# Attention and two mixture-of-experts layers: first expert's weights loaded at its choice, second unit of the second layer fixed one group earlier

## The chip, the cores and the metric

The kernel runs on one core of a Trainium2 chip. That core has TensorE (PE, matrix multiplication), VectorE (DVE), ScalarE (ACT), GpSimd (POOL) and SyncE (SP), which execute their own instruction rows in order and wait for one another by semaphores, and DMA engines that move data between the chip's memory and the core's. The metric is the time of one execution in microseconds (us); lower is better.

## The reference

Attention in two steps over 8 batches, 8 heads and 576 tokens gives x with 4608 rows of 512. Two layers of 8 experts follow. In the first, each expert takes at most 576 tokens, in the order of falling logits; in the second, a token goes to the expert with its largest logit, however many others do.

```python
def _moe_ref(x, w_gate, w1, w2):
    cap = N // E
    logits = x @ w_gate
    order = np.argsort(-logits.flatten())
    for idx in order:
        tok, e = (int(idx) // E, int(idx) % E)
        if assigned[tok] >= 0 or counts[e] >= cap:
            continue
        assigned[tok] = e
        counts[e] += 1
    for e in range(E):
        mask = assigned == e
        out[mask] = np.maximum(x[mask] @ w1[e], 0.0) @ w2[e]

def _moe2_ref(x, modality_id, w_gate, modality_bias, w1, w2):
    logits = x @ w_gate + modality_bias[modality_id]
    e_idx = np.argmax(logits, axis=1)
    gate_w = softmax(logits)[np.arange(N), e_idx]
    for e in range(E):
        mask = e_idx == e
        out[mask] = gate_w[mask, None] * (np.maximum(x[mask] @ w1[e], 0.0) @ w2[e])
```

Here w1 is 512 x 1024 and w2 1024 x 512 for each expert. For these inputs, worked out from the reference, the second layer sends 2308 tokens to one expert and 2300 to another.

## The kernel before

**Attention** handles one batch after the other. ScalarE copies each batch's result to `xm` in five pieces, and five DMAs on SP's row store them to the memory tensor `xs` (L372). The logits of the first layer are made on the way (`LG`), so the routing of the first layer can begin before the last batches are stored.

**Routing of the first layer** runs in eight phases (`class Phases`). Phase k chooses the expert whose list fills next (`choose`, the register tile `R.ex`) and then makes the list of its 576 tokens. A list that fills is found by search steps: VectorE compares (`ge`), TensorE counts (`b`, L654), VectorE folds (`two`, `cp`). `early` (called in attention's last iteration) is the part of the search that needs only the first 20 of the 36 tiles of logits: seven VectorE operations, `best`, `rw`, `mxc`, `sign`, `key`, `digits`.

**Units.** Each expert of the first layer is a unit of 576 tokens (units 0 to 7). The second layer's lists are cut into units of 580 tokens; for these inputs there are eight, called E to E+7 here after their numbers in the code (E is 8). A unit has its weights loaded by SP to the landing tile `raw`, 4 chunks for each of its two weight matrices (L1407, L1428), which are split into a high and a low part by ScalarE (`w1H`, `w2H`, L1460) and mostly VectorE (`w1L`, `w2L`, L1466). GpSimd gathers its tokens to `G` by indirect DMAs (L1263 and L1282), they are transposed to `XT` and split to `XH` and `XL`. Then come the first matrix (`mm`, L1517, three products for each piece), relu and its split `hH` (ScalarE, L1492) and `hL` (VectorE, L1494), the second matrix (L1572), and a store (first layer, `ys`) or an indirect scatter (second layer, `out_dram`, L1344).

**Second layer's lists.** After each expert of the first layer, its 576 results are a "group": the second layer's logits are made, each token is put on the list of its best expert in memory (`lst`, five indirect writes on GpSimd, L973), and counts are kept. `R2.first` fixes unit E after seven of the eight groups: it takes the longest list. After the eighth group `R2.table` places all the other units: an iota on GpSimd (L876), then 24 small VectorE operations, t_s to t_b (L877 to L913). `prepare` loads a unit's expert and list from memory: SP loads `M` and `Mb`, VectorE turns them to gather indices `gi` and scatter indices `si`.

**Order.** The rows of all engines are written out in advance. A planner (`Sched`) holds chains of operations (`cx`, `cw`, `cm` and others), each with a due time, and puts them between the matmuls as its own clock advances. An engine that waits holds all that stands behind it in its row.

Of the kernel before, what the change touches and what calls it, by code (L numbers as in the profile page):

```python
# [59 lines left out]
def attention(tc, ctx, cn, q, k, v, p, w_gate, xs, LG, middle, early):  # L60
# [300 lines left out]
    def out_rows(b, c, ring, hook=None):  # L361
        ahead(b, c)
        n = 128 if c < 4 else 64
        dst = wk.tile([128, 4, 4, 32], F32, name="xm", bufs=5)[:n]
        t = ring.tile([128, 4, 4, 32], F32, name="tr")[:n]
        for g in range(2):
            nc.tensor.matmul(t[:, 2 * g:2 * g + 2], aT[b][:, g, 128 * c:128 * c + n], ops[b][:, g], start=True, stop=True)  # L367
            if hook and not g:
                hook()
        nc.scalar.activation(dst, t.rearrange("p c a i -> p a c i"), AF.Copy)  # L370
        to = xs[b * S:b * S + 512].rearrange("(p m) d -> m p d", m=4)[c] if c < 4 else xs[b * S + 512:(b + 1) * S]
        nc.sync.dma_start(to, dst.rearrange("p a c i -> p (a c i)"))  # L372
        if c == 4:
            del aT[b], ops[b]
# [27 lines left out]
    for i in range(B):  # L402
# [43 lines left out]
        if p1 and SM == 1:  # L446
            sm_max(i - 1)
            sm_sub(i - 1, nc.gpsimd)
        if EARLY and not n1 and EP == 1:
            early()  # L450
        pack_v(i)
        fill(FILL[2])
        pack_D(i)
        if p2 and AT == 0:
            sm_aT(i - 2)
        if AP == 2:
            ahead(*todo[0])
# [156 lines left out]
class Router:  # L614
# [206 lines left out]
class Router2:  # L821
# [39 lines left out]
    def first(self):  # L861
        nc, cn, new = self.nc, self.cn, self.new
        m, t = new("f_m", [128, 1]), new("f_t", [128, E])
        self.fcode, self.fi = new("f_c", [128, 1]), new("f_i", [128, 2], I32)
        nc.vector.tensor_reduce(m, self.cnt, axis=AX.X, op=OP.max)
        nc.vector.scalar_tensor_tensor(t, self.cnt, m, cn["w8"], op0=OP.is_equal, op1=OP.mult)
        nc.vector.tensor_reduce(self.fcode, t, axis=AX.X, op=OP.max)
        self.again = new("f_r", [128, 1])
        nc.vector.tensor_scalar(self.again, m, float(IT), None, op0=OP.is_lt)
        nc.vector.tensor_scalar(self.fi[:, 0:1], self.fcode, -1.0, float(E), op0=OP.mult, op1=OP.add)  # L870
        nc.vector.tensor_scalar(self.fi[:, 1:], self.fcode, -float(LCAP), float(E * LCAP), op0=OP.mult, op1=OP.add)

# [260 lines left out]
EP = 1  # L1133
# [5 lines left out]
RLAG = 2.6  # L1139
IT = 580  # L1140
IG = (IT + 31) // 32
HB = 256
HA = IT - HB
GA = (HA + 31) // 32
RING = 5
NI = (N + E * (IT - 1)) // IT + 1
LCAP = N + -(-IG // 2) * 64


def forward(tc, ctx, cn, R, R2, wg2, S, P, todo, rows, closing, xs, ys, lst, out, m1_w1, m1_w2, m2_w1, m2_w2):  # L1150
    nc = tc.nc
# [9 lines left out]
    def more_phases():  # L1161
        k = phase_k[0]
        if k < E and k <= min(started[0] + 3, P.coded + 2):
            phase_k[0] += 1
            P.add(k)

    for b, c in todo:
# [7 lines left out]
    W = {n: wp.tile([128, 4096], F32R, name="w" + n) for n in ("1H", "1L", "2H", "2L")}  # L1175
    raw = wp.tile([128, 4, 1024], F32, name="raw")
    raws = [raw[:, i] for i in range(4)]
    mp = ctx.enter_context(tc.tile_pool(name="m_ps", bufs=1, space=PSUM))
# [17 lines left out]
    gathered, l1_done, lg_done = [0], [-1], [-1]  # L1196
    free = list(raws)
    queue = []
    landed, due = {}, {}

    class Unit:
# [11 lines left out]
        def ready(self):  # L1213
            if self.one:
                return self.u in P.experts
            return groups[0] >= (7 if self.u == E else 8) and (self.u < E + RING or finished[0] >= self.u - RING)

        def prepare(self):
# [3 lines left out]
            if self.one:  # L1222
                t, i = R.ex, self.u
            elif self.u == E:
                R2.first()
                t, i = R2.fi, 0
            else:
                t, i = R2.tb[:, 0], self.u - E
            self.e = nc.values_load(t[0:1, i:i + 1], engines=[SP], min_val=0, max_val=E - 1)
            if not self.one:  # L1230
                t, i = (R2.fi, 1) if self.u == E else (R2.tb[:, 1], self.u - E)
                off = nc.values_load(t[0:1, i:i + 1], engines=[SP], min_val=0, max_val=(E - 1) * LCAP + N)
# [15 lines left out]
                if self.last:  # L1248
                    cm.ops.append(("vector", 0.1, lambda: nc.vector.tensor_copy(sa, Ma[:, :, 1]), t))
            for which in (1, 2):  # L1250
                queue.extend((self, which, c) for c in range(4))
# [6 lines left out]
        def gather(self):  # L1258
# [139 lines left out]
    def fetch():  # L1398
        while queue and free:
            u, which, c = queue[0]  # L1400
            w = ((m1_w1, m1_w2) if u.one else (m2_w1, m2_w2))[which - 1]
            if which == 1 and (not u.u or 2 <= u.u < BYROW):
                queue.pop(0)
                t = free.pop(0)
                rows = w[bass.ds(u.e, 1)].rearrange("o (c a i) f -> a c i (o f)", a=4, i=32)[c]
                for i in range(4):
                    nc.sync.dma_start(t[32 * i:32 * i + 32], rows[i])  # L1407
                landed[u.u, which, c] = t
                due[u.u, which, c] = S.t["sync"] = max(S.t["sync"], S.t["tensor"] + (2 if u.u else LAND)) + 2.2
                continue  # L1410
# [279 lines left out]
def tile_attention_moe(ctx, tc, q, k, v, p, m1_wg, m1_w1, m1_w2, mod_id, m2_wg, m2_bias, m2_w1, m2_w2, out):  # L1690
# [30 lines left out]
    P.add(0)  # L1721
    forward(tc, ctx, cn, R, R2, wg2, S, P, todo, rows, attn.close, xs, ys, lst, out, m1_w1, m1_w2, m2_w1, m2_w2)

# [21 lines left out]
```

## Time and profile before

| what | value |
|---|---|
| median of 3 runs | 1134.14 us (1133.48 to 1136.73) |
| profiled execution | 1134.52 us |
| its span | 1132.8 us |
| TensorE busy | 1041.8 us, 92% of the span |
| VectorE / GpSimd / ScalarE busy | 713.5 / 488.7 / 444.6 us |
| chain: TensorE, VectorE, issue, DMA, GpSimd | 60%, 12%, 9%, 9%, 5% |
| mean granted clock of TensorE | 0.976 of full |

The span reaches from the first to the last recorded instruction. Busy shares are means over stages with different limits. The chain is followed back from the last instruction, each step to what released it.

### The profile page before, as it was taken

What the parts mean: (1) busy time and instruction counts of PE and PEld (TensorE: products, weight loads), DVE (VectorE), ACT (ScalarE), POOL (GpSimd) and SP (SyncE); (2) the same over time, 40 slices, a digit from 0 to 9 for tenths busy, and PEclk for the clock granted to TensorE, in tenths of its full rate; (3) what the DMA queues carried; (4) which work ended last, traced back from release to release, by engine and by line L of the source; (5) the groups of instructions that cost most, each with busy time, mean ns of one, the idle gap of its engine ahead of it and who ended that gap; (6) DMA issues with size and microseconds to landing.
All of it is one profiled execution on the core that took longest, in us unless ns stands there. A gap on an engine that the chain in (4) does not pass through costs nothing.

```text
span 1132.8 us, 24490 instructions
## 1 busy us (share of the span) xinstructions
PE 1041.8 (92%) x9152; PEld 967.9 (85%) x9152; DVE 713.5 (63%) x2105; ACT 444.6 (39%) x940; POOL 488.7 (43%) x595
## 2 busy tenths in 40 slices
PE   6689797699899998999999999989999999999996
PEld 4577664588888897989999999979898999999995
DVE  1468777688979889884556566655555556455430
ACT  4467564323332323333434334333443433434331
POOL 1123301212424224047565344477787778742401
PEclk9899899699999999999999999999999999999998
DMA  9989246633243242224345343554445454433301
GB/s 257 278 228 259 53 168 201 158 75 117 64 139 113 80 137 57 99 89 145 117 134 138 99 145 93 135 143 126 126 144 143 106 170 136 127 125 102 99 20 43
DMA packets 117857, 146.90 MB, mean 130 GB/s; under 512 B 55946, under 2 KB 80522, under 8 KB 116704
## 3 DMA queue, kind: packets, MB, share of 16 engines
q1 hardware_dynamic: 102368, 116.43, 35.9%
q0 software_dynamic: 13776, 28.76, 8.7%
q8 instruction: 74, 1.21, 0.5%
q14 instruction: 55, 0.45, 0.2%
q10 hardware_dynamic: 1584, 0.05, 0.1%
HBM read 116.31 MB, written 29.52 MB: 129 GB/s over the span
## 4 chain that ended last, share of the span: by engine, by line
PE 60%; DVE 12%; issue 9%; DMA 9%; POOL 5%; ACT 2%; SPq 2%; POOLq 0%; ACTq 0%; DVEq 0%
PE mm L1572 26%; PE mm L1517 22%; DMA G<-ys,gi 4%; POOL out_dram L1344 3%; PE sc L170 2%; POOL G L1282 2%; PE tr L367 1%; DMA raw<-in_moe_w_dram 1%; PE sc L367 1%; DVE hL L1494 1%; DMA G<-xs,idx 1%; DMA vm<-in_v_dram 1%; PE tr L150 1%; DVE cmx L1008 1%; PE b L150 1%
## 5 line engine op out<-in xcount | busy, mean ns | idle before, releaser
L1517 PE MATMUL mm<-XH,w1H 128*128 128x290 f32 (+3 forms) x1024 | 306.9, 300 | 8.7 <-ACT XH L1301 3.8
L1517 PE MATMUL mm<-XL,w1H 128*128 128x290 f32 (+3 forms) x1024 | 307.9, 301 | 0.5 <-DVE XL L1321 0.3
L1517 PE MATMUL mm<-XH,w1L 128*128 128x290 f32 (+3 forms) x1024 | 305.4, 298 | 2.8 <-DVE w1L L1466 2.7
L1572 PE MATMUL mm<-hH,w2H 128*128 128x288 f32 (+3 forms) x768 | 231.9, 302 | 1.1 <-ACT YT L1577 1.1
L1572 PE MATMUL mm<-hH,w2L 128*128 128x288 f32 (+3 forms) x768 | 232.7, 303 | 0.0
L1572 PE MATMUL mm<-hL,w2H 128*128 128x288 f32 (+3 forms) x768 | 231.7, 302 | 0.1
L1492 ACT ACTIVATE hH<-mm 128x290 fp32r<-128x290 f32 (+3 forms) x256 | 105.7, 413 | 293.4 <-PE mm L1517 279.6
L1517 PEld LDWEIGHTS mm<-XH,w1H 128*128 128x128 f32 x1024 | 195.2, 191 | 11.2 <-ACT XH L1301 4.2
L1517 PEld LDWEIGHTS mm<-XH,w1L 128*128 128x128 f32 x1024 | 195.4, 191 | 3.9 <-DVE w1L L1466 3.5
L1517 PEld LDWEIGHTS mm<-XL,w1H 128*128 128x128 f32 x1024 | 194.7, 190 | 1.6 <-DVE XL L1321 0.8
L1494 DVE SCALAR_TENSOR_TENSOR hL<-mm,hH 128x290 fp32r<-128x290 f32 (+3 forms) x256 | 115.2, 454 | 116.7 <-ACT hH L1492 115.6
L1282 POOL DMA_INDIRECT G<-ys,gi x152 | 158.2, 1041 | 62.8 <-issue 31.7
L1572 PEld LDWEIGHTS mm<-hH,w2H 128*128 128x128 f32 x768 | 144.5, 188 | 1.6 <-ACT YT L1577 1.5
L1572 PEld LDWEIGHTS mm<-hL,w2H 128*128 128x128 f32 x768 | 144.5, 188 | 0.3 <-DVE hL L1494 0.3
L1572 PEld LDWEIGHTS mm<-hH,w2L 128*128 128x128 f32 x768 | 144.4, 188 | 0.1
L1344 POOL DMA_INDIRECT out_dram<-Y,si x93 | 96.1, 1033 | 112.0 <-DVE Y L1542 48.5
L1466 POOL TENSOR_TENSOR w2L<-raw,w2H 128x512 fp32r<-128x512 f32 x48 | 63.2, 1338 | 172.2 <-ACT w2H L1460 172.1
L1577 ACT ACTIVATE YT<-mm 128x288 f32<-128x288 f32 (+2 forms) x96 | 39.9, 419 | 203.8 <-PE mm L1572 202.1
L1308 DVE STREAM_TRANSPOSE XT<-G 128x128 f32<-128x128 f32 x206 | 55.6, 295 | 83.6 <-DMA G<-ys,gi 62.0
L1466 DVE TENSOR_TENSOR w1L<-raw,w1H 128x512 fp32r<-128x512 f32 x128 | 83.8, 677 | 19.6 <-ACT w1H L1460 19.0
L1460 ACT ACTIVATE w1H<-raw 128x512 fp32r<-128x512 f32 x128 | 73.1, 623 | 19.5 <-DMA raw<-in_moe_w_dram 11.5
L1460 ACT ACTIVATE w2H<-raw 128x512 fp32r<-128x512 f32 x128 | 73.1, 622 | 0.0
(383 smaller groups left out, 1544.3 us busy)
## 6 DMA issues: line engine op xcount, KB each, us to landing
raw<-in_moe_w_dram SPq DMA_DIRECT2D x112, 512.0 KB
ys<-Y SPq DMA_DIRECT2D x8, 1152.0 KB
qm<-in_q_dram SPq DMA_DIRECT2D x8, 1024.0 KB
vm<-in_v_dram SPq DMA_DIRECT2D x8, 1024.0 KB
xs<-xm SPq DMA_DIRECT2D x32, 256.0 KB
raw<-in_moe_w_dram SPq DMA_DIRECT2D x64, 128.0 KB
km<-in_k_dram SPq DMA_DIRECT2D x7, 1024.0 KB
G<-ys,gi POOLq DMA_INDIRECT x152
```

Of the source, the lines that this page charges most:

```text
L150: nc.tensor.transpose(t[:, i, :], src[:, h + i // 2, 128 * (i % 2):128 * (i % 2) + 128], ident)
L170: nc.tensor.matmul(t[32 * c:32 * c + 32, :512].rearrange("p (i j n) -> p j i n", i=2, j=2)[:, j], lhs(h, j), m[:, h], start=True, stop=Tru ...
L1282: nc.gpsimd.indirect_dma_start(out=G[:, g], out_offset=None, in_=ys[:n], in_offset=bass.IndirectOffsetOnAxis(ap=self.gi[:, g:g + 1], axis= ...
L1308: nc.vector.transpose(out=self.x[0][:, :, 32 * g:32 * g + 32], in_=G[:, g].rearrange("p (c i) -> p c i", c=4))
L1344: i = nc.gpsimd.indirect_dma_start(out=to, in_=rows, in_offset=None, out_offset=bass.IndirectOffsetOnAxis(ap=at, axis=0), bounds_check=to. ...
L1460: nc.scalar.activation(a, b, AF.Copy)
L1466: (nc.gpsimd if pool else nc.vector).tensor_tensor(p[0], p[1], p[2], op=OP.subtract)
L1492: nc.scalar.activation(hh, t, AF.Relu)
L1494: ch.ops.append(("vector", 0.37, lambda: nc.vector.scalar_tensor_tensor(hl, t, 0.0, hh.bitcast(F32), op0=OP.max, op1=OP.subtract), ts + 0.2))
L1517: nc.tensor.matmul(t, a[:, c, fs], b[:, c, s], start=(i == 0), stop=(i == 11))
L1572: nc.tensor.matmul(t, l, r, start=(i == 0), stop=(i == 23))
L1577: nc.scalar.activation(YT[:, d, s], t, AF.Copy)
```

## The change

Four things are edited. First, `raw` is taken from a pool that exists all the time, not from one opened after attention is closed; a hook on `choose` (`first_loads`) issues unit 0's 16 first-matrix loads on SP as soon as the first expert is chosen, and the five stores of the last batch go from SP's row to ScalarE's. Second, `early` is called behind `pack_v`, `pack_D` and `sm_aT`. Third, `PRE = 2`: `R2.first` fixes two units after seven groups, E and the next 580 tokens of the same list (for these inputs the lists of both experts hold 2016 tokens then, so `again`, which would void the early choice on a short list, stays zero), and `prepare` and the gathers of E+1 follow E's; its gathers read only the rows of the first seven groups. Fourth, with one more unit that may be needed, `NI` grows from 16 to 17, and the rows of the table from 128 to 136 numbers.

```diff
-        nc.sync.dma_start(to, dst.rearrange("p a c i -> p (a c i)"))
+        (nc.scalar if b == B - 1 else nc.sync).dma_start(to, dst.rearrange("p a c i -> p (a c i)"))
...
-        if EARLY and not n1 and EP == 1:
-            early()
         pack_v(i)
         fill(FILL[2])
         pack_D(i)
         if p2 and AT == 0:
             sm_aT(i - 2)
+        if EARLY and not n1 and EP == 1:
+            early()
...
+        for i in range(2, PRE + 1):
+            nc.vector.scalar_tensor_tensor(self.again, m, float(IT * i), self.again, op0=OP.is_lt, op1=OP.add)
...
+        for i in range(PRE):
+            nc.vector.tensor_scalar(self.fi[:, 1 + i:2 + i], self.fcode, -float(LCAP), float(E * LCAP + IT * i), op0=OP.mult,
+                                    op1=OP.add)
...
+PRE = 2
...
-NI = (N + E * (IT - 1)) // IT + 1
+NI = (N + E * (IT - 1)) // IT + PRE
...
+    def load_rows(u, e, c, t):
+        w = m1_w1 if u < E else m2_w1
+        rows = w[bass.ds(e, 1)].rearrange("o (c a i) f -> a c i (o f)", a=4, i=32)[c]
+        for i in range(4):
+            nc.sync.dma_start(t[32 * i:32 * i + 32], rows[i])
+        landed[u, 1, c] = t
+        due[u, 1, c] = S.t["sync"] = max(S.t["sync"], S.t["tensor"] + (2 if u else LAND)) + 2.2
+
+    def first_loads():
+        if one_e or 0 not in P.experts:
+            return
+        one_e.append(nc.values_load(R.ex[0:1, 0:1], engines=[SP], min_val=0, max_val=E - 1))
+        for c in range(4):
+            load_rows(0, one_e[0], c, raws[c])
+
+    P.hooks.append(first_loads)
...
-    raw = wp.tile([128, 4, 1024], F32, name="raw")
-    raws = [raw[:, i] for i in range(4)]
...
-            return groups[0] >= (7 if self.u == E else 8) and (self.u < E + RING or finished[0] >= self.u - RING)
+            return groups[0] >= (7 if self.u < E + PRE else 8) and (self.u < E + RING or finished[0] >= self.u - RING)
...
-                t, i = (R2.fi, 1) if self.u == E else (R2.tb[:, 1], self.u - E)
+                t, i = (R2.fi, 1 + self.u - E) if self.u < E + PRE else (R2.tb[:, 1], self.u - E)
...
-                t = S.t["tensor"] + (CM0 if self.u == E else CM1)
+                t = S.t["tensor"] + (CM0 if self.u < E + PRE else CM1)
...
-            n = 4 * (N - CAP if self.u == E else N)
+            n = 4 * (N - CAP if self.u < E + PRE else N)
...
-            if g > E and g + 1 < limit[0]:
+            if g >= E and g + 1 < limit[0]:
                 units[g + 1].prepare()
...
+    raw = rp.tile([128, 4, 1024], F32, name="raw")
```

Line numbers move by the change (L1466 becomes L1483, L1494 becomes L1511, L1282 becomes L1304). The rows below are read without times: they are the order of the instructions.

SP's row at the end of attention, before: the stores of the last two batches (L372), then the load of the chosen expert's number and the first weights (L1407).

```order
L372 DMA xs<-xm 128x512 x4
L372 DMA xs<-xm 64x512
L372 DMA xs<-xm 128x512 x4
L372 DMA xs<-xm 64x512
L1229 TENSOR_LOAD ex
L1229 ISA x2
L1407 ISA
L1407 DMA raw<-in_moe_w_dram 32x1024
```

After the change, at the same place:

```order
L372 DMA xs<-xm 128x512 x4
L372 DMA xs<-xm 64x512
L372 DMA xs<-xm 128x512 x4
L372 DMA xs<-xm 64x512
L1186 TENSOR_LOAD ex
L1186 ISA x2
L1179 ISA
L1179 DMA raw<-in_moe_w_dram 32x1024
```

The last batch's five stores have left the row, and the weights follow the stores of the batch before it.

GpSimd's row at the second layer's start, before: the gathers of E (`gi_2490`), the last group's five list writes, two of which stand here, the iota, the gathers of E+1 (`gi_2491`), the first scatter of E.

```order
L1282 DMA G<-ys,gi_2490 128x128 x19
L973 DMA lst<-pay,r2d 41984x4
L975 MEMSET spacer 1x1
...
L973 DMA lst<-pay,r2d 41984x4
L975 MEMSET spacer 1x1
L876 IOTA t_i 1x16
L1282 DMA G<-ys,gi_2491 128x128 x19
L1344 DMA out_dram<-Y,si_2495 18432x128
```

After the change (`gi_2516` is E, `gi_2517` is E+1, `gi_2513` is E+2):

```order
L1304 DMA G<-ys,gi_2516 128x128 x19
L1304 DMA G<-ys,gi_2517 128x128 x19
L977 DMA lst<-pay,r2d 41984x4
L979 MEMSET spacer 1x1
...
L977 DMA lst<-pay,r2d 41984x4
L979 MEMSET spacer 1x1
L880 IOTA t_i 1x17
L1304 DMA G<-ys,gi_2513 128x128 x19
```

E+1's gathers have moved ahead of the five list writes and the iota; behind the iota now stand E+2's gathers, which were behind twelve of E's scatters.

VectorE's row while unit E is in its first matrix, before: the eighth of the sixteen `hL` of this matrix, the table from `t_s` to `t_b`, and the three `hL` that follow it.

```order
L1494 SCALAR_TENSOR_TENSOR hL<-mm_2464,hH 128x290
L1466 TENSOR_TENSOR w2L<-raw,w2H 128x4x4x32
L877 TENSOR_SCALAR t_s<-t_i 1x16
L878 TENSOR_SCALAR t_e<-w_351 1x8
...
L913 CAST t_b<-t_y 1x32
L1466 TENSOR_TENSOR w2L<-raw,w2H 128x4x4x32
L1494 SCALAR_TENSOR_TENSOR hL<-mm_2465,hH 128x290
L1494 SCALAR_TENSOR_TENSOR hL<-mm_2466,hH 128x290
L1494 SCALAR_TENSOR_TENSOR hL<-mm_2467,hH 128x290
```

After the change:

```order
L1483 TENSOR_TENSOR w2L<-raw,w2H 128x4x4x32
L1511 SCALAR_TENSOR_TENSOR hL<-mm_2489,hH 128x290
L881 TENSOR_SCALAR t_s<-t_i 1x17
L882 TENSOR_SCALAR t_e<-w_352 1x8
...
L917 CAST t_b<-t_y 1x34
L1511 SCALAR_TENSOR_TENSOR hL<-mm_2490,hH 128x290
L1511 SCALAR_TENSOR_TENSOR hL<-mm_2491,hH 128x290
L1511 SCALAR_TENSOR_TENSOR hL<-mm_2492,hH 128x290
L1549 MEMSET YT 128x4x28
```

The table has moved down to between the thirteenth and the fourteenth `hL` of unit E; three of the sixteen stand behind it, where eight stood before.

## Rows read from the trace of the kernel before

**Rows 1.** The page of before, its head: span and number of instructions.
```profile
span 1132.8 us, 24490 instructions
```

**Rows 2.** Windows from:to: length; busy us of each engine (instructions); clock; DMA; GB/s.
```profile
185.00:193.00 8.00, 4.68 (x56) 3.38 (x54) 7.10 (x31) 2.95 (x5) 0.00 (x0) 1.00 0.51 170
190.00:215.00 25.00, 8.00 (x54) 6.01 (x44) 16.36 (x56) 6.60 (x12) 7.53 (x7) 0.57 0.85 219
755.51:762.00 6.49, 6.22 (x32) 5.92 (x33) 4.85 (x8) 4.12 (x8) 5.39 (x10) 0.74 0.48 89
762.00:770.00 8.00, 8.00 (x62) 8.00 (x61) 3.77 (x11) 3.11 (x7) 6.50 (x12) 1.00 0.43 145
```

**Rows 3.** Chain of work, 183 to 219: start us, us, what.
```profile
189.34 3.44 DMA xs<-xm
...
192.92 0.38 SPq L1407
...
203.26 6.70 DMA raw<-in_moe_w_dram
...
213.27 5.79 PE mm L1517 x32
```

**Rows 4.** Timeline of VectorE (DVE) near 183: start us, us, instruction.
```profile
183.35 0.15 DVE L1008 TENSOR_SCALAR ex<-code 128x1 int32<-128x1 f32 x1
```

**Rows 5.** Timeline of TensorE (PE): second half of E, first matmul of E+1.
```profile
729.34 0.32 PE L1572 MATMUL mm<-hL,w2H 128*128 128x324 f32 x1
...
755.51 0.40 PE L1517 MATMUL mm<-XH,w1H 128*128 128x290 f32 x1 [3.58 <-ACT XH L1325]
```

**Rows 6.** Timeline of GpSimd (POOL): gathers of E, E+1, E+2, list writes, iota.
```profile
694.12 1.00 POOL L1282 DMA_INDIRECT G<-ys,gi  x1 [0.30 <-issue]
709.18 1.02 POOL L973 DMA_INDIRECT lst<-pay,r2d  x1 [14.06 <-DVE pay L1008]
...
715.69 0.14 POOL L876 IOTA t_i<- 1x16 f32 x1
...
726.93 1.05 POOL L1282 DMA_INDIRECT G<-ys,gi  x1 [11.10 <-DVE si L1247]
...
750.76 1.21 POOL L1282 DMA_INDIRECT G<-ys,gi  x1 [0.30 <-issue]
...
768.52 1.05 POOL L1282 DMA_INDIRECT G<-ys,gi  x1 [0.23 <-issue]
```

**Rows 7.** Waits, 700 to 870: total us, times, longest.
```profile
PE mm L1517 <- ACT XH L1325: 3.6, 1, 3.6
...
PE mm L1517 <- DVE w1L L1466: 2.7, 2, 1.9
...
PE mm L1517 <- DVE hL L1494: 1.3, 1, 1.3
```

**Rows 8.** Timeline of ScalarE (ACT): copies of the last batch.
```profile
187.13 1.19 ACT L370 ACTIVATE xm<-tr 128x512 f32<-128x512 f32 x2 [0.54 <-PE tr L367]
```

**Rows 9.** Timelines near 132: one row of VectorE, GpSimd and TensorE each.
```profile
132.64 2.13 DVE L671 TENSOR_TENSOR rw<-LG,best 128x160 bf16<-128x160 f32 x1
...
132.46 2.13 POOL L323 TENSOR_TENSOR T<-T,mx 128x1152 f32<-128x1152 f32 x1 [1.97 <-DVE mx L319]
...
136.34 0.66 PE L250 MATMUL tr<-ident,dup 128*128 128x128 f32 x2 [3.02 <-DVE dup L242]
```

**Rows 10.** Waits of TensorE for search steps: 180 to 262, then 213.2 to 262.
```profile
PE b L654 <- DVE ge L1008: 10.8, 5, 3.1
...
PE b L654 <- DVE ge L1008: 1.3, 1, 1.3
```

**Rows 11.** Timeline of VectorE: the table from first to last, and hL.
```profile
715.87 0.16 DVE L877 TENSOR_SCALAR t_s<-t_i 1x16 f32<-1x16 f32 x1 [0.39 <-POOL t_i L876]
...
721.03 0.17 DVE L913 CAST t_b<-t_y 1x32 int32<-1x32 f32 x1
...
721.73 0.44 DVE L1494 SCALAR_TENSOR_TENSOR hL<-mm,hH 128x290 fp32r<-128x290 f32 x1
```

More of the change, by code (lines that the diff above doesn't have):

```diff
@@ L863, in first @@
         m, t = new("f_m", [128, 1]), new("f_t", [128, E])
-        self.fcode, self.fi = new("f_c", [128, 1]), new("f_i", [128, 2], I32)
+        self.fcode, self.fi = new("f_c", [128, 1]), new("f_i", [128, 1 + PRE], I32)
         nc.vector.tensor_reduce(m, self.cnt, axis=AX.X, op=OP.max)
@@ L869, in first @@
         nc.vector.tensor_scalar(self.again, m, float(IT), None, op0=OP.is_lt)
+        for i in range(2, PRE + 1):
+            nc.vector.scalar_tensor_tensor(self.again, m, float(IT * i), self.again, op0=OP.is_lt, op1=OP.add)
         nc.vector.tensor_scalar(self.fi[:, 0:1], self.fcode, -1.0, float(E), op0=OP.mult, op1=OP.add)
-        nc.vector.tensor_scalar(self.fi[:, 1:], self.fcode, -float(LCAP), float(E * LCAP), op0=OP.mult, op1=OP.add)
+        for i in range(PRE):
+            nc.vector.tensor_scalar(self.fi[:, 1 + i:2 + i], self.fcode, -float(LCAP), float(E * LCAP + IT * i), op0=OP.mult,
+                                    op1=OP.add)
     def table(self):
@@ L1145, with forward @@
 RING = 5
-NI = (N + E * (IT - 1)) // IT + 1
+NI = (N + E * (IT - 1)) // IT + PRE
 LCAP = N + -(-IG // 2) * 64
-def forward(tc, ctx, cn, R, R2, wg2, S, P, todo, rows, closing, xs, ys, lst, out, m1_w1, m1_w2, m2_w1, m2_w2):
+def forward(tc, ctx, cn, R, R2, wg2, S, P, raw, todo, rows, closing, xs, ys, lst, out, m1_w1, m1_w2, m2_w1, m2_w2):
     nc = tc.nc
@@ L1165, in more_phases @@
             P.add(k)
+    raws = [raw[:, i] for i in range(4)]
+    queue, landed, due, one_e = [], {}, {}, []
+    def load_rows(u, e, c, t):
[12 more added lines that the diff above has]
+    P.hooks.append(first_loads)
     for b, c in todo:
@@ L1196, in forward @@
     gathered, l1_done, lg_done = [0], [-1], [-1]
-    free = list(raws)
-    queue = []
-    landed, due = {}, {}
+    free = []
     class Unit:
@@ L1223, in prepare @@
                 t, i = R.ex, self.u
-            elif self.u == E:
-                R2.first()
+            elif self.u < E + PRE:
+                if self.u == E:
+                    R2.first()
                 t, i = R2.fi, 0
@@ L1228, in prepare @@
                 t, i = R2.tb[:, 0], self.u - E
-            self.e = nc.values_load(t[0:1, i:i + 1], engines=[SP], min_val=0, max_val=E - 1)
+            self.e = (nc.values_load(t[0:1, i:i + 1], engines=[SP], min_val=0, max_val=E - 1) if self.u
+                      else one_e[0])
             if not self.one:
-                t, i = (R2.fi, 1) if self.u == E else (R2.tb[:, 1], self.u - E)
+                t, i = (R2.fi, 1 + self.u - E) if self.u < E + PRE else (R2.tb[:, 1], self.u - E)
                 off = nc.values_load(t[0:1, i:i + 1], engines=[SP], min_val=0, max_val=(E - 1) * LCAP + N)
@@ L1249, in prepare @@
                     cm.ops.append(("vector", 0.1, lambda: nc.vector.tensor_copy(sa, Ma[:, :, 1]), t))
-            for which in (1, 2):
+            for which in (1, 2) if self.u else (2,):
                 queue.extend((self, which, c) for c in range(4))
@@ L1401, in fetch @@
             w = ((m1_w1, m1_w2) if u.one else (m2_w1, m2_w2))[which - 1]
-            if which == 1 and (not u.u or 2 <= u.u < BYROW):
+            if which == 1 and 2 <= u.u < BYROW:
                 queue.pop(0)
[L1404 to L1409, printed above, removed]
+                load_rows(u.u, u.e, c, free.pop(0))
                 continue
@@ L1721, in tile_attention_moe @@
     P.add(0)
-    forward(tc, ctx, cn, R, R2, wg2, S, P, todo, rows, attn.close, xs, ys, lst, out, m1_w1, m1_w2, m2_w1, m2_w2)
+    forward(tc, ctx, cn, R, R2, wg2, S, P, raw, todo, rows, attn.close, xs, ys, lst, out, m1_w1, m1_w2, m2_w1, m2_w2)
 _INS = ["q", "k", "v", "p", "moe_w_gate", "moe_w1", "moe_w2", "moe2_modality_id", "moe2_w_gate", "moe2_modality_bias",
```

## The prediction

> **What bounds the kernel now.** I read the span first, then a table of windows to find stretches in which TensorE is not full, then the chain and the waits inside them. The profiled execution takes 1134.52 us: 1132.8 of span [rows 1] and 1.7 outside it. It lies 0.4 above the median of 1134.14, so a sum against it is lowered by 0.4 at the end.
>
> Two places with idle TensorE touch this change. The first is the border between attention and the first layer's first unit: in 190 to 215 TensorE works 8.00 of 25 us, at a mean granted clock of 0.57, between its levels of 1.2 and 2.4 GHz [rows 2]. The reader is to see in the chain why [rows 3]: the last store of attention's output (`xs<-xm`) lands at 189.34 + 3.44 = 192.78. Only then does SP begin, at 192.92, to issue the first expert's first-layer weights. The last two links of them end at 203.26 + 6.70 = 209.96, and the first matmul run without gaps starts 3.3 us later, at 213.27. Yet the expert that these weights depend on was written at 183.35 [rows 4]. SP waited 9.6 us longer, for memory and for list work, not for the choice.
>
> The second place is the turn between the second layer's first two units (E and E+1 below). TensorE stands 3.58 us at 755.51 for XH, the transposed tokens [rows 5]. After that it goes on slowly: from 755.51 to 762 it does 32 matmuls, where the next 8 us hold 62, or 0.129 us each [rows 2]. 32 of these are 4.13 us, so 2.36 of the 6.49 are lost; 0.27 of that is a short second wait, and 2.1 is the clock, 0.74 of full in this window. The cause stands on GpSimd's row: E+1's 19 gathers run only from 726.93 to 750.76 [rows 6], since their unit was fixed after the eighth group. All waits of TensorE for weights and tokens between 700 and 870 are 3.6 (XH), 2.7 (w1L) and 1.3 (hL) [rows 7].
>
> **Part 1, early first weights.** Their landing memory no longer overlays attention's, so the 16 transfers may follow the choice. On SP's row they stand behind batch 6's stores. The last five stores, batch 7's, leave SP for ScalarE's queue. Two copies of `xm` took 1.19 us with 0.54 of waiting ahead of them [rows 8], 0.87 each; five of them end at 189.3, so batch 6's last store should be issued near 185, and I let the weights start then, not at 183.35.
>
> What they get of the DMA engines decides. From 185 to 193 these were busy 0.51 of the time [rows 2], 4.1 us of eight. The weights are 16 x 131 KB = 2.1 MB; at 219 GB/s, the rate of the crowded stretch [rows 2], they need 9.6 us. Two of the five gathers are needed for the first matmuls, 128 tokens of 2 KB each: 0.52 MB, 2.4 us. One after the other, with the 4.1 already occupied, that is 16.1 us from 185, so 201.1 if the engines never idle, and 3.3 us later TensorE starts: 204.4. A second way gives a bound. Before, the engines were as good as full from 194 to 210; the spare time from 185 to 193 (8 - 4.1 = 3.9 us) is taken off, and the last weights land at 206.1, with matmuls from 209.4. The other bound is 202, with xs free of any delay and TensorE ready sooner than 3.3 us after landing. I take 206 before part 2, nearer to the first way, since the second lets second-layer weights pass that need not. Gain 213.3 - 206 = 7.3, bounds 3.9 and 11.3.
>
> Issue costs: five DMA issues move from SP to ScalarE. An issue on SP took 0.38 us in the chain [rows 3]; five are 1.9 us on an engine that waits there for TensorE's transposes between its copies. I take nothing; without that cover the last store is up to 1.9 late, which is inside the bounds.
>
> **Part 2, `early` behind the packing.** Seven VectorE operations for the first list leave the front of `dup` and `qm` in attention's last iteration. One, `rw`, took 2.13 us from 132.64, and TensorE waited 3.02 until 136.34 for `dup` [rows 9]. Afterwards `dup` can run before 132.64, but `qm` reads what GpSimd writes until 132.46 + 2.13 = 134.59 [rows 9]. `qm` stands right behind `dup` and began near 136.34, so its chain moves by 1.8, and the seven operations fall behind it, where the next transposes may wait 0.1 for them. I take 1.8; bounds 0 (a later wait eats it) and 3.0 (the whole wait). Everything behind it moves, so first matmuls come near 204.2.
>
> **Part 3, the planner's reshuffle.** Two more of the eight search steps of the second list now stand behind the first matmul. Inside matmul time the whole first unit had one wait for such a step, 1.3 us [rows 10]; I charge 0.5 for each, 1.0 in all, bounds 0 and 3. Parts 1 to 3: 7.3 + 1.8 - 1.0 = 8.1.
>
> **Part 4, the second unit fixed early.** The seven-group counts hold more than two units on the longest list, so the two units are useful ones: no work is added. E+1's 19 gathers now follow E's directly on GpSimd. E's last gather starts at 694.12 [rows 6] and 19 more at 1.32 us (726.93 to 750.76 is 18 steps) end near 720.5. The turn of E+1 can then be done 30 us before it is needed, and 3.6 + 0.3 + 2.1 = 6.0 us go.
>
> But the five list writes and the iota go behind these gathers. They took from 709.18 to 715.69, 6.5 us [rows 6], so the iota comes at 727.0, not 715.69. The table that places all later units follows it on VectorE: from 715.87 to 721.20, 5.3 us [rows 11]. Afterwards that is 727.2 to 732.5. On VectorE's row the table stands ahead of the last three hL, and second-layer matmuls read the seventh pair's hL at 729.34 [rows 5]. Three hL at 0.44 [rows 11] end at 732.9, 733.4 and 733.8; so TensorE waits 3.6 for the first of them, and about 0.4 more for the last. A gap of 3.6 cost 2.1 of clock above; the same is due here. The new loss is 4.0 + 2.1 = 6.1, and what E+1's turn gave is paid back: -0.1. Bounds for the stall: nothing (if E's gathers run earlier against TensorE than before) and 9 (if the last group's list work is 3 us later still).
>
> What remains as gain: E+2's gathers, at 768.52 before, can begin once the table is read and the list loaded, near 739 (6 us behind the table, as 726.93 lay behind 721.20). Each later unit starts ahead by so much that the other waits, w1L 2.7 and hL 1.3, which come from VectorE waiting for gathers, should go: 4.0, bounds 0 and 5.5 (if such waits that only share in a stall go too). Part 4 is 3.9.
>
> The added VectorE operations (one each in comparing and in placing) are some 0.2 us ahead of E's list and hidden behind first-layer matmuls; uncovered they are 0.4. The extra conditional unit is not entered, and its test costs nothing that another test does not show.
>
> **Sum.** 8.1 + 3.9 = 12.0: 1134.5 - 12.0 = 1122.5, less 0.4: 1122.1.
>
> **The rivals.**
> *No table stall.* If GpSimd gets to the iota 4 us sooner against TensorE, hL is not late and 6.1 come on top: 1116.0. For it: before, TensorE began E 4 us after E's last gather, and the start of this layer may shift against the gathers. Against it: the rows in order are fixed, and 19 gathers are 25 us.
>
> *Half of it is eaten.* The first weights and the last xs stores run on the same DMA engines. If the stores are slowed as much as the weights gain, tokens are late and part 1 gives 3.9 or less; then 1125.5. Or the later waits stay, since they come from VectorE's own order: 1126.1. Both: 1129.5. For it: the engines are at 0.85 over 190 to 215 [rows 2]. The Trainium skill speaks for this one: its page "DMA: Bandwidth & Descriptors", section "Issuing engines are not separate DMA queues", says that transfers begun by different engines run on the same 16 DMA engines and interleave, and that a further issuing engine saves only issue time. By that rule the move to ScalarE's queue shields the stores from nothing. No row of before has weights and stores in flight together, so the trace can't yet say.
>
> *The change does not do what it says.* If a wait on SP other than the memory holds the first weights until 192.9, part 1 is nothing and the stores' move alone stays; with parts 2 to 4 as forecast it ends at 1129.4. SP's row speaks against it.
>
> *Slower.* Search steps inside matmul time. Six of the eight now stand there. While TensorE was idle one such wait lasted up to 3.1 us [rows 10]. If each of six stops TensorE as long, that is 18.6, and the 1.3 of before and the 1.0 charged come off: 16.3 more, against 12.0, so 1138.4. The sign turns at (12.0 + 2.3) / 6 = 2.4 us for each step, and from 3.0 on it is slower by over 0.3%; against it stands that four steps cost 1.3 together before.
>
> **Chances.** Forecast, within 3 us: 0.45. No stall: 0.17. Half eaten, either way: 0.24. Not doing what it says: 0.07. So much lost that it ends within 0.3% of before (3.4 us, about what a measurement of this kernel can tell from no change): 0.04. Slower: 0.03. The range reaches from 1114 (no stall, and a start 2 us better) to 1129; beyond lie one in ten above and less below. Faster 0.93, same 0.04, slower 0.03.
>
> **What would show it.** Right: the first weights issued near 185 and landed by 202; the first full matmul run between 202 and 207; no wait for XH at E+1; a wait of TensorE for hL of about 4 us some 3 us into E's second half, with a half clock behind it; E+2's gathers ahead of E+1's matmuls. Wrong: xs landing later than 192 and a wait for tokens in its place; iota ahead of E's last first-layer matmuls; waits for w1L of 1 us or more after E+1; search waits over 1 us inside the first unit.

## The result, and the profile after

The changed kernel takes 1121.82 us (1121.21 to 1122.21, four runs) where the one before takes 1133.85 beside it: the ratio is 0.9864, 95% interval 0.9833 to 0.9895. That is faster by more than 0.3%, and 0.3 us from the forecast of 1122.1. The span of the profiled execution is 1119.7, so 13.1 shorter; the medians differ by 12.0, since the two profiled executions lie on opposite sides of theirs. Some executions on a chip are slower at a lower granted clock; the ratios leave these out and the medians don't.

Where the 13.1 lie is read from three points of TensorE's timeline: the first product with `XL` (the first matmul run without gaps, 213.27 in [rows 3]), the first matmul of unit E, and the end. Two rows of before that were not needed so far, the first matmuls of E and of E+4 (columns: start us, us, engine, line, instruction, and in brackets the idle time ahead of it and what ended it):

```profile
698.89 0.30 PE L1517 MATMUL mm<-XH,w1H 128*128 128x290 f32 x1
...
916.52 0.30 PE L1517 MATMUL mm<-XH,w1H 128*128 128x290 f32 x1
```

The same timeline of the changed kernel:

```profile
204.62 0.58 PE L1534 MATMUL mm<-XH,w1H 128*128 128x256 f32 x1 [0.69 <-ACT XH L1323]
...
205.35 0.58 PE L1534 MATMUL mm<-XL,w1H 128*128 128x256 f32 x1
...
689.33 0.40 PE L1534 MATMUL mm<-XH,w1H 128*128 128x290 f32 x1 [1.27 <-ACT XH L1347]
...
725.42 0.64 PE L1589 MATMUL mm<-hL,w2H 128*128 128x324 f32 x1 [4.84 <-DVE hL L1511]
...
750.09 0.30 PE L1534 MATMUL mm<-XH,w1H 128*128 128x290 f32 x1
...
903.43 0.30 PE L1534 MATMUL mm<-XH,w1H 128*128 128x290 f32 x1
```

The start gives 213.27 - 205.35 = 7.9. The first layer itself, from there to E's first matmul, took 485.62 and takes 483.98, so 1.6 less. From E to the end it was 1132.8 - 698.89 = 433.9 and is 1119.7 - 689.33 = 430.4: 3.5. Together 13.0; the rest is rounding.

**The start.** The chain of work from attention's end, in the changed kernel (start us, us, what):

```profile
184.93 5.33 DMA xs<-xm
...
192.99 2.33 DMA raw<-in_moe_w_dram
...
195.38 1.52 POOL G L1285
...
197.21 5.56 DMA G<-xs,idx
...
202.82 1.13 PE mm L1322 x4
...
203.97 0.61 ACT XH L1323
...
204.62 6.25 PE mm L1534 x36
```

The reader is to see that the weights are no longer its last link, as in [rows 3]. The tokens are. The last store, issued at 187.07, landed at 194.13 by the landing records of the trace: 7.06 us, where the last one took 3.44 before. The first gather began at 195.38, and the gathered tokens took another 5.56. The profile puts the gather's wait down to a weight load that landed at 195.32, just before it; but in six traces (before, changed, e3, e6c, e7, e8) the first gather begins 0.9 to 1.3 us behind the landing of the last store, whatever the loads do, so the stores are what it waits for. The loads' issue on SP, from its timeline, was drawn out too:

```profile
183.78 12.71 SPq L1179 DMA_DIRECT2D raw<-in_moe_w_dram  x16
```

They start at 183.78 instead of 192.92 and end their issue 12.7 us later, where the same sixteen took 10.65 before. SP itself waited for stores to land in between (all its waits of this kind from 180 to 206: total us, times, longest):

```profile
SPq L1179 <- DMA xs<-xm: 3.0, 3, 2.2
```

**The second layer.** All waits of TensorE from 680 to 860 (total us, times, longest); of the three of [rows 7], w1L is gone, XH stands at E and not at E+1, and hL is now one long wait in E:

```profile
PE mm L1589 <- DVE hL L1511: 4.8, 1, 4.8
PE mm L1534 <- ACT XH L1347: 1.3, 1, 1.3
PE mm L1534 <- DVE XL L1343: 0.3, 1, 0.3
```

GpSimd's timeline, to be laid beside [rows 6]:

```profile
711.70 1.00 POOL L1304 DMA_INDIRECT G<-ys,gi  x1 [0.30 <-issue]
713.00 1.02 POOL L977 DMA_INDIRECT lst<-pay,r2d  x1 [0.30 <-issue]
...
719.41 0.15 POOL L880 IOTA t_i<- 1x17 f32 x1
731.50 1.05 POOL L1304 DMA_INDIRECT G<-ys,gi  x1 [11.94 <-DVE si L1269]
```

VectorE's, beside [rows 11]:

```profile
719.60 0.17 DVE L881 TENSOR_SCALAR t_s<-t_i 1x17 f32<-1x17 f32 x1 [1.89 <-POOL t_i L880]
...
724.84 0.17 DVE L917 CAST t_b<-t_y 1x34 int32<-1x34 f32 x1
724.93 1.17 DVE L1511 SCALAR_TENSOR_TENSOR hL<-mm,hH 128x290 fp32r<-128x290 f32 x3
```

The list writes now follow the 38 gathers of E and E+1 without a pause, the iota comes at 719.41, the table waits for it and ends at 725.01, and the three hL follow. TensorE stands 4.84 us until 725.42. The window behind shows the clock (columns as in [rows 2]):

```profile
720.00:730.00 10.00, 5.16 (x21) 4.89 (x21) 9.45 (x33) 1.83 (x4) 0.00 (x0) 0.67 0.25 45
```

### The profile page after: what moved, and what is told of

It is laid out like the page before. It is cut to its first block, busy times and chain, and to the rows that moved or that the text cites. A ratio compares the mean times of both kernels' runs of the same rounds, so it can differ in the third digit from the quotient of the medians.

```text
span 1119.7 us, 24511 instructions
## 1 busy us (share of the span) xinstructions
PE 1039.8 (93%) x9152; PEld 966.3 (86%) x9152; DVE 707.3 (63%) x2107; ACT 444.6 (40%) x940; POOL 491.3 (44%) x595
## 4 chain that ended last, share of the span: by engine, by line
PE 69%; DVE 11%; issue 7%; DMA 6%; POOL 3%; ACT 2%; SPq 2%; POOLq 0%; ACTq 0%; DVEq 0%
PE mm L1589 30%; PE mm L1534 26%; PE sc L170 2%; PE tr L367 1%; POOL G L1304 1%; DMA G<-xs,idx 1%; DMA G<-ys,gi 1%; PE tr L150 1%; DVE hL L1511 1%; PE sc L367 1%; PE mm L1322 1%; DMA vr<-in_v_dram 1%; POOL lst L977 1%; DVE ge L1012 1%; PE b L654 1%
## 5 line engine op out<-in xcount | busy, mean ns | idle before, releaser
L1304 POOL DMA_INDIRECT G<-ys,gi x152 | 161.9, 1065 | 67.7 <-issue 28.7
L1511 DVE SCALAR_TENSOR_TENSOR hL<-mm,hH 128x290 fp32r<-128x290 f32 (+3 forms) x256 | 115.5, 454 | 119.1 <-ACT hH L1509 118.1
L1483 POOL TENSOR_TENSOR w2L<-raw,w2H 128x512 fp32r<-128x512 f32 x48 | 61.7, 1306 | 153.1 <-ACT w2H L1477 153.0
L1594 ACT ACTIVATE YT<-mm 128x288 f32<-128x288 f32 (+2 forms) x96 | 40.1, 419 | 216.0 <-PE mm L1589 210.2
L1483 DVE TENSOR_TENSOR w1L<-raw,w1H 128x512 fp32r<-128x512 f32 x128 | 83.6, 677 | 20.6 <-ACT w1H L1477 19.9
L1285 POOL DMA_INDIRECT G<-xs,idx x25 | 25.2, 1008 | 111.0 <-DMA raw<-in_moe_w_dram 53.5
```

What stands on the lines that cost most here:

```text
L1285: nc.gpsimd.indirect_dma_start(out=r.rearrange("p a d -> p (a d)"), out_offset=None, in_=xs, in_offset=bass.IndirectOffsetOnAxis(ap=phases ...
L1304: nc.gpsimd.indirect_dma_start(out=G[:, g], out_offset=None, in_=ys[:n], in_offset=bass.IndirectOffsetOnAxis(ap=self.gi[:, g:g + 1], axis= ...
L1483: (nc.gpsimd if pool else nc.vector).tensor_tensor(p[0], p[1], p[2], op=OP.subtract)
L1511: ch.ops.append(("vector", 0.37, lambda: nc.vector.scalar_tensor_tensor(hl, t, 0.0, hh.bitcast(F32), op0=OP.max, op1=OP.subtract), ts + 0.2))
L1594: nc.scalar.activation(YT[:, d, s], t, AF.Copy)
```

## The experiments

On the chips that took the first ten runs TensorE paused again and again from about 300 us on, so that the kernel before took 1354 to 1366 us there. The changed kernel itself was not run on them. Their totals are compared only with the kernel before on the same chip, and what they show of the start is read from intervals inside each trace. For five traces alike in this part (changed, e4, e4b, e6, e6c) the sum, in the table's last column, lies between 72.7 and 73.2. In e1 and e1b, alike too, it is 73.81 and 73.45; there the clock was half for a while, which the part on the prediction comes back to.

These intervals, in us, are from the timelines. The first is from the start of the last `mx` of L319 on VectorE to the end of attention's last copy to `xm`; the next three are from that end; the last is the sum from `mx` to the first product with XL. That `mx` stands at 131.10 before and 132.19 after, and between 126 and 132 in the other traces, though nothing ahead of it was edited, so times are counted from it.

| kernel | mx to last copy | first load issued | first gather | first XL product | sum |
|---|---|---|---|---|---|
| before | 58.21 | +3.61 | +4.38 | +23.96 | 82.17 |
| changed | 54.85 | -3.26 | +8.34 | +18.31 | 73.16 |
| e2, `early` in front | 58.16 | -3.27 | +8.33 | +18.10 | 76.26 |
| e3, weights behind stores | 54.31 | +2.04 | +4.54 | +22.52 | 76.83 |
| e7, weights in two halves | 56.18 | -4.58 | +3.68 | +18.48 | 74.66 |
| e6c, table spread | 54.85 | -3.25 | +7.52 | +17.83 | 72.68 |
| e8, two batches' stores moved | 55.81 | -6.03 | +5.64 | +15.55 | 71.36 |

**`early` back in front** (e2).

```diff
+        if EARLY and not n1 and EP == 1:
+            early()
         pack_v(i)
...
-        if EARLY and not n1 and EP == 1:
-            early()
         if AP == 2:
```

> Changed kernel with the seven operations of the first list back in front of the packing. Theory (attention's chain carries them, so its end and all behind it move): attention's last copy about 2 us later, 1123.6 to 1124.2 us. Rival (the first matmuls wait for DMA traffic that is full anyway, so an earlier end of attention is not seen): within 0.7 us of the changed kernel's 1121.8.

Attention's last copy comes 3.3 us later (58.16 against 54.85), and the first product with XL with it, 3.1 later. That is the theory's side. The rival is not wholly out: in e1 and e1b the last copy comes 1.7 later than with the change (56.58 and 56.57), but the first XL product only 0.65 and 0.3. Its total was 1358.48 against 1365.71 before, ratio 0.9946 (0.9916 to 0.9975), on a chip that can't settle 2 us.

**Weights behind the stores** (e3): the memory's move alone.

```diff
-        (nc.scalar if b == B - 1 else nc.sync).dma_start(to, dst.rearrange("p a c i -> p (a c i)"))
+        nc.sync.dma_start(to, dst.rearrange("p a c i -> p (a c i)"))
...
-    P.hooks.append(first_loads)
...
+    S.until(lambda: 0 in P.experts)
+    first_loads()
     closing()
```

> Changed kernel with the last batch's stores back on SP's row and the first weights behind them: only the memory's move is left, the loads need not wait for the stores to land. Theory (weights and stores share the DMA engines, so what the weights gain by going first the tokens lose): stores land near 190.5 instead of 195, gathers start near 191.5, weights land some 2 us later than with the change, first unbroken matmuls within 1.5 us of 204.6, 1120.5 to 1123.5 us. Rival (the weights are what is waited for, each us of their start counts): issued 4 us later, first matmuls near 208.5, 1125.5 us.

Tokens came as early as the theory said (first gather 4.54 behind the last copy, as in the kernel before), but the first product with XL came 4.2 later than with the change: the rival's number. Its chain of work ends in the weights again (start us, us, what):

```profile
196.24 7.49 DMA raw<-in_moe_w_dram
...
203.84 0.64 ACT w1H L1478
...
204.50 1.29 DVE w1L L1484 x2
205.79 1.21 DVE XL L1325 x2
```

Its last store took 3.61 us to land, about as before (3.44; 7.06 with the change). So of the 5.65 us that the change gains behind attention's end, the memory alone gives 1.4, and that the loads go ahead of the stores gives 4.2, although the stores pay for it. Ratio 0.9961 (0.9927 to 0.9995).

**Weights in two halves** (e7): eight loads as with the change, eight on ScalarE's row behind the last stores.

```diff
-        for c in range(4):
+        for c in range(2):
             load_rows(0, one_e[0], c, raws[c])
...
+    for c in (2, 3):
+        load_rows(0, one_e[0], c, raws[c], nc.scalar)
     closing()
```

> Changed kernel with the first weights in two halves: eight loads on SP's row as before, eight behind the last batch's stores on ScalarE's row. Theory (weights and stores share the DMA engines, and the tokens came last by it): the first gather 2 us sooner after attention's last copy (8.3 us with the change), first unbroken matmuls about 1 us sooner (17.6 with the change), 1120.8 us. Rival (the weights' own issue time is what counts, as four us lost in the run with the weights behind the stores): first matmuls 1 to 2 us later, 1123 us.

Half right. The first gather comes 4.7 us sooner behind the last copy, more than expected, and the last store took 2.6 us to land instead of 7.06, so the weights in flight are what held the stores. But the first XL product doesn't come sooner (18.48 against 18.31): the chain passes to VectorE, which has search steps and w1L in one row.

```profile
200.49 0.60 DVE w1L L1486
201.10 0.26 DVE cmx L1012
...
202.19 1.89 DVE w1L L1486 x3
204.08 1.21 DVE XL L1327 x2
205.33 1.86 PE mm L1537 x7
```

Attention's end came 1.3 later as well; that ScalarE reads the expert's number too in this kernel may be why, which was not tested. Ratio 1.002 (1.0 to 1.0039).

**One unit early** (e1, e1b): `PRE = 2` becomes `PRE = 1`, and `NI` with it 16 again.

```diff
-PRE = 2
+PRE = 1
```

> Changed kernel with one unit fixed after seven groups, as before; the start is that of the changed kernel. Theory (the start gains some 8.6 us by its own, the second unit's early choice gives a net 3 to 4 us because its gain at E+1 is paid back as a wait for hL): about 1125.5 us, first unbroken matmuls again near 204.6, no hL wait of 4.8 us in E, and a wait for XH of about 3.6 us at E+1 with a half clock behind it. Rival (the early unit gives most of the 12 us, the start little): 1130 or more.

> The kernel of the first run once more, since TensorE stood in long gaps of its own there from about 300 us on. Theory: about 1125.5 us where the kernel before takes 1134, no hL wait in E, an XH wait of about 3.6 us at E+1. Rival (the early unit gives most of the gain): 1130 or more.

1352.06 against 1365.71 (ratio 0.9888, 0.9857 to 0.9918) and 1345.14 against 1358.14 (0.9901, 0.9866 to 0.9937). As shares these are the theory's 0.992 or better, but e4b, with the same start, took as long as the kernel before on the chip of e1b, so these totals can't say what the start gives. In the second layer TensorE was so slow that neither the XH wait at E+1 nor the hL wait could be seen. Inconclusive for the second unit.

**The iota ahead of the gathers** (e4, e4b). `steps` makes `t_i` and `t_s` when the first two units are fixed.

```diff
                     R2.first()
+                    R2.steps()
...
+    def steps(self):
+        nc, new = self.nc, self.new
+        i23, st = new("t_i", [1, NI]), new("t_s", [1, NI])
+        nc.gpsimd.iota(i23, pattern=[[1, NI]], base=0, channel_multiplier=0, allow_small_or_imprecise_dtypes=True)
+        nc.vector.tensor_scalar(st, i23, float(IT), None, op0=OP.mult)
```

> Changed kernel with the iota (and the multiplication behind it) made when the first two units are fixed, ahead of the gathers; VectorE's order is otherwise the same, the table still ahead of the last three hL. Theory (the table is late since the iota stands behind 19 gathers and five list writes): the wait of TensorE for hL falls from 4.8 to about 2.9 us, that is the 1.9 us for which the table waited for the iota; 1119 to 1120.5 us, less if the short gap also spares the clock. Rival (the 5.3 us of the table itself behind the gathers' landing are the whole of it, or the list writes hold it): wait of 4 us or more, 1121.5 us.

> The iota made ahead of the gathers, once more. Theory: the hL wait in E falls from 4.8 to about 2.9 us (the table's own 5.3 us still stand ahead of the last three hL), 1119 to 1120.5 us. Rival (the list writes or the table alone hold VectorE): wait of 4 us or more, 1121.5 us.

1357.17 against 1365.71 (0.9928, 0.9887 to 0.997) and 1360.61 against 1358.14 (1.0022, 0.999 to 1.0054): one kernel, 0.7% under and 0.2% over the one before, so the totals settle nothing. There is no hL wait at all in either trace: E's first matrix lasted 29.6 us instead of 28.1, and the table was done 31.5 us behind E's start instead of 35.7. Nor is there one in e2, e3 and e7, which have the changed kernel's second layer. Neither theory nor rival is touched by that.

**The table planned one by one as well** (e6, e6c), and **with one more batch's stores on ScalarE's row** (e8).

```diff
             def done():
                 groups[0] += 1
-                if self.u == E - 1:
-                    R2.table()
                 gather_next()
...
+            if self.u == E - 1:
+                R2.table()
             R2.nc = nc
```

For e8, in addition:

```diff
-        (nc.scalar if b == B - 1 else nc.sync).dma_start(to, dst.rearrange("p a c i -> p (a c i)"))
+        (nc.scalar if b >= B - 2 else nc.sync).dma_start(to, dst.rearrange("p a c i -> p (a c i)"))
```

> As the one before, and the table's operations planned one by one, so that the last three hL stand between them instead of behind them. Theory (the wait in E is only VectorE's order): no hL wait over 1 us in E, no half clock behind it, E+2's gathers still done before E+2 is needed: 6 to 7 us under the changed kernel, 1115 to 1116 us. Rival (the wait goes to E+1 or E+2, since the table is ready later): a wait for XH or gi at E+2 of 2 us or more, 1118 us or more.

> Iota ahead of the gathers and the table planned one by one, once more, for a chip on which TensorE isn't gated in the second layer. Theory (the hL wait is only VectorE's order behind a late iota): no hL wait over 1 us in E and no half clock behind it, 1115 to 1116 us where the kernel before takes 1134. Rival (the wait goes to E+2, whose list and gathers come later): 1118 us or more.

> As the one before, and the stores of the last batch but one on ScalarE's row too, so that SP reads the first expert as soon as it is written. Theory (the start is set by when the DMA engines get the weights' work, since they are full up to the first matmul): loads issued 5 to 6 us ahead of attention's last copy instead of 3.3, first matmuls some 2 us sooner after it (about 15.5 against 17.6), 1.5 to 2 us under the one before. Rival (the last stores are slowed by as much): first matmuls at 17 us or more, no difference.

e6 took 1339.74 against 1358.14 (0.9868, 0.9823 to 0.9913), e6c 1345.79 against 1354.22 (0.9918, 0.9881 to 0.9956), e8 1345.41 against the same (0.9931, 0.9903 to 0.9959). The second layer can't be judged by these. The start of e8 can: loads are issued 6.0 us ahead of the last copy, the first XL product follows 15.55 behind it, and the sum from `mx` is 1.3 shorter than in e6c, though the five further issues on ScalarE cost attention 1.0. The theory's side, less than its 1.5 to 2.

**Lighter first units** (f1, f2): units 0 to 5 leave out the products with the low parts, in the hope that TensorE, less worked, would not pause in the second layer (first matrix here, the second likewise). f1 is otherwise the changed kernel, f2 has the early iota and the table planned one by one.

```diff
                 for a, b in ((wh, xh), (wl, xh), (wh, xl)):
-                    nc.tensor.matmul(t, a[:, c, fs], b[:, c, s], start=(i == 0), stop=(i == 11))
+                    if u.u >= LEAN or i % 3 == 0:
+                        nc.tensor.matmul(t, a[:, c, fs], b[:, c, s], start=(i == 0), stop=(i == (11 if u.u >= LEAN else 9)))
```

> The changed kernel, but units 0 to 5 leave out two of the three products of each matrix (the low parts), so that TensorE has worked less when the second layer begins and is not gated there as in the runs before; everything from unit 6 on is whole, and the instructions of the other engines are the same in the same order. Its own total says nothing of the change. Theory and rival alike: in E a wait for hL of 4 to 5 us, behind a table that begins when the iota is done.

> The same lighter first units, with the iota ahead of the gathers and the table's operations planned one by one. Theory (the hL wait is VectorE's order behind a late iota, and the half clock after it its consequence): no hL wait over 1 us in E, a full clock there, no wait of 1 us or more at E+1 and E+2, and a time 6 to 7 us under that of the run beside it. Rival (the wait moves to E+2's tokens): a wait for XH at E+2 of 2 us or more, 3 us or less under it.

The chip ran the kernel before, with nothing left out, at 1136.74, so that the lighter units are what kept TensorE from pausing is not shown. The second layer stood as in the changed kernel. TensorE's timeline in f1, the start of E and the hL wait:

```profile
676.21 0.40 PE L1536 MATMUL mm<-XH,w1H 128*128 128x290 f32 x1 [1.19 <-ACT XH L1348]
...
712.54 0.64 PE L1592 MATMUL mm<-hL,w2H 128*128 128x324 f32 x1 [5.08 <-DVE hL L1512]
```

The same in f2, the starts of E and E+1 and the longest wait behind them:

```profile
670.33 0.40 PE L1541 MATMUL mm<-XH,w1H 128*128 128x290 f32 x1 [0.55 <-ACT XH L1353]
...
723.85 0.30 PE L1541 MATMUL mm<-XH,w1H 128*128 128x290 f32 x1
...
829.64 0.40 PE L1541 MATMUL mm<-XH,w1L 128*128 128x290 f32 x1 [1.56 <-DVE w1L L1489]
```

In f1 E's first matmul is 61.5 us ahead of E+1's (737.69), as in the changed kernel (60.8); in f2 it is 53.5, so 8.0 less. The hL wait is gone there, and the clock in E is full. But from E to the end f1 takes 1107.0 - 676.21 = 430.8 and f2 1096.9 - 670.33 = 426.6: 4.2 less, not 6 to 7. The rest is given back, 2.6 of it in E+3 (826.99 to 880.73, so 53.7 us where it is 51.1 in f1), where TensorE waits 2.1 for w1L at 829.64 and just after. f2's table ends 39.6 us behind E's start and f1's 35.9, so the table's lateness alone doesn't stop TensorE; that the three hL stand behind it does. Whether the early iota was needed as well is not shown, since f2 has both edits. Neither expectation is met in full: the wait in E is VectorE's order, as the theory says, but half of the gain goes into later waits, of another kind than the rival's. The totals, 1103.35 (1098.83 to 1108.77) and 1101.43 (1098.66 to 1108.48), scatter too much to show 4 us.

## Why the prediction was right

**The start.** Forecast: 7.3 for the early weights, 1.8 for `early`, -1.0 for the reshuffled search steps. Measured from `mx` on: behind attention's end 23.96 - 18.31 = 5.65, ahead of it 58.21 - 54.85 = 3.36, in the first layer +1.6; up to `mx`, where nothing was edited, this trace is 1.1 longer. Their forecast sum was 8.1, and E starts 9.6 earlier. The early weights worked as forecast but for the stores; the premise of the second term was wrong, and in the first layer 1.6 came where 1.0 was charged. That forecast and result lie 0.3 us apart is luck: the terms were off by 1 to 3 us each, in both directions.

The term for the weights was too large by the part of the rival "half of it is eaten" that came true: loads at 183.78 (forecast near 185) and weights landed by 199.6 (forecast by 202), but the last store beside them landed at 194.13, the gather began 8.34 behind the last copy instead of 4.38, and tokens became the last link. Among the signs listed as wrong this one, "xs landing later than 192 and a wait for tokens in its place", is what the trace shows. e3 and e7 show that the weights did it, and e7 that VectorE would have come next. The five issues that moved to ScalarE, charged nothing, cost attention's end 0.5 (54.85 against 54.31 in e3). By the rule cited from the Trainium skill ("DMA: Bandwidth & Descriptors", section "Issuing engines are not separate DMA queues") the move to ScalarE's row would shield the stores from nothing; the trace agrees, 7.06 us for the last store, which took 3.44.

The term for `early` rests on a wrong reading. By it `qm` had to wait for the GpSimd operation that ends at 134.59 in [rows 9]. That operation works on the `T` of another batch (`sm_sub(i - 1)` in the kernel, where `qm` is `sm_aT(i - 2)`), and in the changed kernel `qm` begins while it runs:

```profile
134.03 1.37 DVE L338 STREAM_TRANSPOSE qm<-T 128x1152 f32<-128x1152 f32 x1
...
133.56 2.13 POOL L323 TENSOR_TENSOR T<-T,mx 128x1152 f32<-128x1152 f32 x1 [1.97 <-DVE mx L319]
```

So `qm` moved ahead by 3.4 us (1.84 behind the start of `mx` instead of 5.27), not by 1.8, and the scores by 2.3 (5.52 instead of 7.83). Then there is a clock that I had left out: the granted clock was 0.50 from 136 to 142 before, behind the wait of 3.02 in [rows 9], and 1.00 from 136 to 140 after. In e1, with the same order and the same gaps, it was 0.60 from 139 to 142, and attention's end came 1.7 later than after the change (56.58 against 54.85); e1b and f1 show the same. So the order by itself gave 1.6 of the 3.36, and that this is near the forecast's 1.8 is luck; the 1.7 of the clock came in this trace and didn't in those.

```profile
136.00:139.00 3.00, 1.87 (x41) 1.48 (x44) 1.74 (x3) 0.76 (x2) 0.00 (x0) 0.50 0.02 5
139.00:142.00 3.00, 3.00 (x52) 2.62 (x47) 2.65 (x8) 0.00 (x0) 0.00 (x0) 0.50 0.00 0
```

These are windows of before (columns as in [rows 2]). The changed kernel's answer to them, then e1's:

```profile
136.00:139.00 3.00, 1.85 (x60) 1.40 (x58) 2.75 (x11) 1.53 (x3) 0.00 (x0) 1.00 0.00 0
137.50:140.00 2.50, 2.40 (x63) 1.91 (x64) 2.32 (x7) 0.05 (x1) 0.00 (x0) 1.00 0.00 0
...
139.00:142.00 3.00, 3.00 (x43) 2.06 (x34) 2.18 (x5) 0.00 (x0) 1.42 (x1) 0.60 0.00 0
```

**Search steps.** Charged 1.0, they cost nothing net: the first layer is 1.6 shorter, and all waits of TensorE for search and list steps in it fell from 18.2 to 14.6 us. What made them fall was not tested.

**The second layer.** The step that the gain at E+1 is paid back in E held: forecast 4.0 of wait for hL and 2.1 of clock, measured 4.84 of wait. The windows from E's first matmul to E+1's, before and after:

```profile
698.89:755.51 56.62, 53.04 (x380) 50.10 (x378) 37.10 (x121) 19.20 (x43) 28.10 (x35) 1.00 0.46 125
...
689.33:750.09 60.76, 55.65 (x378) 52.58 (x379) 42.76 (x136) 21.77 (x46) 38.50 (x43) 0.94 0.48 126
```

Without the XH wait of 3.58 that ended it before, this stretch was 53.04 long, so 7.7 us were lost there: 4.84 for hL, 0.27 for XL at E's start, and 2.6 more of TensorE's own time for the same matmuls, at a clock of 0.94 instead of 1.00. That is more than the 6.1 forecast; the iota came 30.1 us behind E's first matmul, where the forecast put it 28.1 behind. f2 takes the wait away, and with it 8.0 us of E. What remains as gain was too small in the forecast: from E+1's start to E+4's, 916.52 - 755.51 = 161.0 before and 903.43 - 750.09 = 153.3 after, 7.7 us, of which 2.4 are E+1's own slow begin; 5.3 against a forecast of 4.0. The forecast counted the waits for w1L and hL that went, and not the lower clock behind them: TensorE's own time for these 1009 matmuls fell from 156.6 to 153.3, and only 2.1 of that belong to E+1's begin. The two errors cancel, which is luck: 3.5 measured, 3.9 forecast. E+2's gathers began at 731.50, 42.2 us behind E's first matmul; the forecast's 739, on the axis of before, is 40.1 behind it.

**The rivals.** "Half of it is eaten" was right that the stores pay, but the early weights gave 5.65, not 3.9 or less, and the later waits went; "no table stall" fell (4.84); "not doing what it says" fell (183.78); "slower" fell, with no search wait over 0.6 us in the first unit.

## What to carry to other kernels

A load that is let go earlier does not gain its whole head start: here it was issued 6.9 us sooner behind attention's end and gave 5.65. What runs beside it pays, so look which transfer ends last afterwards (here the tokens) before sizing the gain. Work that moves ahead in one engine's row pushes back whatever depended on that row without being named in the change: here an iota, and through it a table and three small operations that TensorE needs. The gaps of 3.0, 3.6 and 4.8 us in TensorE's work here cost their length and then a stretch at a lower clock. A move that shortens such a gap gives back the length; the clock it may give back or not, as the changed kernel and e1 show at 136 to 142. Before a wait is charged to an engine's operation, check in the code that the two share a buffer and not only a name.

## What the runs showed of the hardware

On two of the three chips of these runs TensorE stood in pauses of its own: in e7's trace, from 300 on, its waits without a releaser were (total us, times, longest)

```profile
PE mm L1592 <- issue: 91.7, 92, 2.4
PE mm L1537 <- issue: 61.1, 69, 2.4
```

at a mean granted clock of 0.88 from there on, while on the third chip the same kernel before took 1136.7. The totals there don't follow the intervals of the table (e1b and e6 took 1345 and 1340, e4b and e7 1361 and 1359, on one chip); why stays open.

VectorE's `rw` took 2.13 us when it began 0.18 behind a GpSimd operation of 2.13 us ([rows 9]), and ended 0.18 behind it; e2 shows the same. In the changed kernel it took 0.33, from 135.63, where that operation ends at 133.56 + 2.13 = 135.69. The Trainium skill says of the port pair that the two engines share, on its page "SBUF — State Buffer", section "SBUF: two separate sides", that it is an exclusive lock held for the whole instruction; these two durations agree with it.
